# A second level of seven products in the w_out half of an attention and SiLU kernel

## The chip, the cores and the metric

The kernel runs on one core of a Trainium2 chip. The metric is the device time of one execution in microseconds (us). Executions of one kernel agree within 0.4% here (before 1540.95 to 1544.35); ratios are taken within runs that were made together on the same chip. In the profile PE is TensorE, PEld its weight loads, DVE VectorE, ACT ScalarE, POOL GpSimd, SP the engine that issues the DMAs. The granted clock is the share of TensorE's full speed that the chip allowed at a time. To evict or empty a bank is to copy a finished product out of PSUM, and an operation is held (off) when it stands still until another engine's operation ends.

## The reference

```python
# q, k, v: (8, 12, 448, 64)
q_n, k_n = rmsnorm(q, g_q), rmsnorm(k, g_k)
attn = softmax(scale * q_n @ k_n.T)             # per batch and head
x = (attn @ v).transpose(0, 2, 1, 3).reshape(3584, 768)
h = x @ w_in                                    # 768 x 2048
g = h / (1 + exp(-h))
out = g @ w_out                                 # 2048 x 768, float32
```

The change concerns the last line, and how `g` ("hidden") is stored for it.

## The kernel before: the parts that matter

Each large product is done in Winograd's form of Strassen's method: both operands are cut into four blocks, and seven block products with some sums of blocks take the place of eight. The left operand's sums are s1, s2, s4, the right one's t1, t2, t4. `seven` runs the products and adds them up as they come out of PSUM:

```python
def seven(left, right, steps, n, done):
    ...
    p1, u2, u3, p5 = (parts[:, ds(i * S, n)] for i in range(4))
    nc.scalar.copy(p1, (yield from product("1")))
    plus((yield from product("2")), p1, done[1, 1])
    plus((yield from product("6")), p1, u2)
    nc.scalar.copy(p5, (yield from product("5")))
    plus((yield from product("7")), u2, u3)
    nc.gpsimd.tensor_tensor(out=u2, in0=u2, in1=p5, op=ALU.add)
    nc.gpsimd.tensor_tensor(out=done[2, 2], in0=u3, in1=p5, op=ALU.add)
    plus((yield from product("3")), u2, done[1, 2])
    plus((yield from product("4")), u3, done[2, 1])

def bank(n):                      # a product's PSUM bank: two in turn
    return ps.tile([P, BANK], F32, name="mm", bufs=2)[:, 0:n]
```

The kernel lays out eight PSUM banks. In attention two are `mm`, one `tr`, one `av`, and four hold scores, as two tiles of two banks (one bank per head):

```python
def scores(n, half):
    for j in range(2 * half, 2 * half + 2):
        banks = ps.tile([R, 2, BANK], F32, name="sc", bufs=2)
        ...
```

The kernel has three stages. In the first (to about 860 us) attention runs pair by pair of heads, with the w_in product of the batches already done as a filler. In the second (to 1028 us) the last two batches' w_in product runs while w_out is loaded, rounded and summed (`prepare_out`). In the third, 14 tiles of 256 tokens are each multiplied with all of w_out: `left_sums`, then `seven` with 8 steps of 384 columns, then the stores.

Of the kernel before, what the change touches and what calls it, by code (L numbers as in the profile page):

```python
# [168 lines left out]
def kernel(  # L169
# [19 lines left out]



    nc = tc.nc
    z = Shapes(q, w_in)
    P, D, R, J = z.P, z.D, z.R, z.J
# [108 lines left out]
    )  # L303


def store(nc, out, z, column, o, m0):


    at = 0
    while at < o.shape[0]:  # L310
        b, c = divmod(column + at, z.S)
        j, p = divmod(c, z.R)
        n = min(z.R - p, o.shape[0] - at)
        rows = out[ds(b * z.S, z.S), ds(m0, o.shape[1])].rearrange("(p j) m -> j p m", j=z.J)
        nc.sync.dma_start(rows[j, ds(p, n)], o[ds(at, n), :])
        at += n

# [2 lines left out]
def bounded(  # L320
# [17 lines left out]
        return parts  # L338


    hidden = dram.tile([z.NF, P, z.B * S], F32, name="hidden")


    sets = [mem.tile([P, 2 * z.NW * S], F32, name=f"x{i}") for i in range(2)]
    sums_x = mem.tile([P, 3 * HW * S], F32, name="sums_x")
    NSTAGE = 3
    stage = mem.tile([P, NSTAGE * 2 * S], F32, name="stage")
    parts = mem.tile([P, 4 * S], F32, name="parts")
    work = mem.tile([P, 15 * S + 2 * J * D], F32, name="work")
    qT0, qT1, kT, e0, e1, e2, e3, es, xU, r = divided(  # L350
# [12 lines left out]
    def normalise(n):  # L363
        if n <= last:
            normalise_rows(
                nc, z, state[n], normal[n % 2], squares, rms[n % 4], minus_half, nc.gpsimd
            )
# [22 lines left out]
    def scores(n, half):  # L390

        for j in range(2 * half, 2 * half + 2):
            banks = ps.tile([R, 2, BANK], F32, name="sc", bufs=2)
            for h in range(2):
                rows = ds(h * D, D)
                nc.tensor.matmul(  # L396
                    banks[:, h, 0:S], kT[rows, ts(j, R)], qT[n % 2][rows, :],
                    start=True, stop=True,
                )
            for h in range(2):  # L400
                nc.scalar.activation(  # L401
                    e[j][:, h, :], banks[:, h, 0:S], AF.Exp, scale=rms[n % 4][:, 1, h, j : j + 1]
                )
# [35 lines left out]
    def minus(a, b, out):  # L439
        nc.vector.tensor_tensor(out=out, in0=a, in1=b, op=ALU.subtract)  # L440

    def plus(a, b, out):
        nc.vector.tensor_tensor(out=out, in0=a, in1=b, op=ALU.add)  # L443

    def left_sums(a11, a12, a21, a22, s1, s2, s4, steps=range(4)):

        for step in steps:
            (
                lambda: plus(a21, a22, s1),
                lambda: minus(s1, a11, s2),  # L450
                lambda: minus(a11, a21, a21),
                lambda: minus(a12, s2, s4),
            )[step]()

    def right_sums(b11, b12, b21, b22, t1, t2, t4):

        minus(b12, b11, t1)
        minus(b22, t1, t2)
        minus(b22, b12, b12)
        minus(b21, t2, t4)  # L460

    def bank(n):
        return ps.tile([P, BANK], F32, name="mm", bufs=2)[:, 0:n]

    def seven(left, right, steps, n, done):



        def product(name):
            t = bank(n)  # L470
            for i, s in enumerate(steps):
                nc.tensor.matmul(  # L472
                    t, left(name, s), right(name, s), start=i == 0, stop=i == len(steps) - 1
                )
                yield n
            return t

        p1, u2, u3, p5 = (parts[:, ds(i * S, n)] for i in range(4))
        nc.scalar.copy(p1, (yield from product("1")))  # L479
        plus((yield from product("2")), p1, done[1, 1])  # L480
        plus((yield from product("6")), p1, u2)
# [5 lines that stand above are left out]
        plus((yield from product("4")), u3, done[2, 1])  # L487


    stages = 0  # L490

    def staged():
        nonlocal stages
        stages += 1
        return stage[:, ts((stages - 1) % NSTAGE, 2 * S)]

    def save(f, column, t):
        nc.sync.dma_start(hidden[f, :, ds(column, t.shape[1])], t)

    def whole(b, blocks):  # L500

        for f in blocks:
            h = bank(S)
            assert room.w_in.rounded >= (f // room.CHUNK + 1) * z.NW
            for c in range(z.NW):
                nc.tensor.matmul(  # L506
                    h, room.w1(c, f), xT(b, c), start=(c == 0), stop=(c == z.NW - 1)
                )
                yield S
            t = staged()[:, 0:S]  # L510
            nc.scalar.activation(t, h, AF.Silu)
            save(f, b * S, t)

    summed = set()

# [22 lines left out]
    def halves_in(group, blocks, beside=lambda m: iter(())):  # L538
        owed = []
        for m in blocks:  # L540
# [21 lines left out]
            done = {(i + 1, j + 1): rows[i][:, ts(j, S)] for i in range(2) for j in range(2)}  # L562
            aside = beside(m)
            count = 0
            for columns in seven(lambda name, c: lefts[name](c), right, range(HW), S, done):
                count += 1
                if count % HW == 1:
                    if count > HW:
                        activate(owed)
                    next(aside, None)  # L570
                yield columns
            for _ in aside:
                pass
            owed = [(2 * m + i, group[0], rows[i]) for i in range(2)]
        activate(owed)

    def activate(owed):
        for f, b, t in owed:
            nc.scalar.activation(t, t, AF.Silu)
            save(f, b * S, t)  # L580
        owed.clear()



# [24 lines left out]
    def chunk_out(i):  # L609

        w = home[i][0].rearrange("p (m r h k) -> p m r h k", m=2, r=2, h=2)
        s = home[i][1].rearrange("p (s m k) -> p s m k", s=3, m=2)
        return (
            w[:, :, 0, 0], w[:, :, 0, 1], w[:, :, 1, 0], w[:, :, 1, 1], s[:, 0], s[:, 1], s[:, 2]
        )

    def prepare_out(m):

        if m == 0:
            fetch(0)  # L620
        for _ in range(room.CHUNK):
            rounder.open()
            yield
            rounder.round()
        if m % 2:
            right_sums(*chunk_out(ORDER[m // 2]))
        yield

    NT = z.B * S // P
    size = z.NF * 2 * P  # L630
    tiles = [work[:, ds(0, size)], sets[1][:, ds(0, size)]]
    s_tiles = [work[:, ds(size, 3 * HF * P)], sums_x[:, ds(0, 3 * HF * P)]]
    outs = [stage[:, ds(i * z.DM, z.DM)] for i in range(3)]
    outs += [room.chunk(3)[:, ts(i, z.DM)] for i in range(3)]

    def fetch(t):

        if t >= NT // 2:
            return
        dst = tiles[t % 2].rearrange("p (f c) -> p f c", f=z.NF)  # L640
        nc.sync.dma_start(
            dst, hidden[:, :, ds(t * 2 * P, 2 * P)].rearrange("f p c -> p f c")
        )

    def halves_out(t):
        w = tiles[t % 2].rearrange("p (m r t c) -> p m r t c", m=HF, r=2, t=2)
        s = s_tiles[t % 2].rearrange("p (s m c) -> p s m c", s=3, m=HF)
        a11, a12, a21, a22 = (w[:, :, i, j] for j in range(2) for i in range(2))
        left_sums(a11, a12, a21, a22, s[:, 0], s[:, 1], s[:, 2])
        lefts = {"1": a11, "2": a12, "3": s[:, 2], "4": a22, "5": s[:, 0], "6": s[:, 1], "7": a21}  # L650

        def right(name, m):
            b11, b12, b21, b22, t1, t2, t4 = chunk_out(m // 2)
            return {"1": b11, "2": b21, "3": b22, "4": t4, "5": t1, "6": t2, "7": b12}[name][
                :, m % 2
            ]

        o = [outs[(2 * t + i) % len(outs)] for i in range(2)]
        done = {(i + 1, j + 1): o[i][:, ts(j, z.HALF)] for i in range(2) for j in range(2)}
        steps = [2 * i + k for i in ORDER for k in range(2)]  # L660
        yield from seven(lambda name, m: lefts[name][:, m], right, steps, z.HALF, done)
        for i in range(2):
            if t < NT // 2 - 1 or i == 0:
                store(nc, out, z, (2 * t + i) * P, o[i], 0)
            else:
                for j in (1, 0):
                    store(nc, out, z, (2 * t + i) * P, o[i][:, ts(j, z.HALF)], j * z.HALF)


    filler = dict(work=iter(()), due=0.0, share=0.0)  # L670

    def begin(work, columns, parts):
        finish()
# [11 lines left out]
    def finish():  # L685
        for _ in filler["work"]:
            pass
# [34 lines left out]
    for n in range(last + 2):  # L722
# [40 lines left out]
            fill()  # L763
        weights_in(n, 3)
        normalise(n + 3)
    finish()
    fetch(1)
    for t in range(NT // 2):
        for _ in halves_out(t):
            pass  # L770
        fetch(t + 2)


@with_exitstack
# [208 lines left out]
```

## Time and profile before

| | us |
|---|---|
| median of 9 runs, over all comparisons | 1543.4 (1540.95 to 1544.35) |
| profiled run: span | 1539.4 |
| start of the last reciprocal but one of attention | 859.1 |
| first matmul of the third stage | 1027.7 |
| end of its last matmul | 1533.7 |

The three last rows are read from the instructions in order of time, and they cut the span into four stretches: attention (859.1), preparation (168.6), w_out product (506.0) and end (5.7). The lines behind this are shown in the prediction.

### The profile page before, as it was taken

To read this page: it belongs to the slowest core of one execution; us is meant where nothing else is said; L and a number is where in the kernel's file an instruction comes from. 1 tells how busy PE (TensorE), PEld (TensorE's weight loads), DVE (VectorE), ACT (ScalarE), POOL (GpSimd) and SP (SyncE) were. 2 spreads that over 40 slices of the span, in tenths; PEclk is the share of its full clock that TensorE was granted. 3 is DMA by queue.
4 is the path that set the end of the run, shared out by engine and by line. 5 is a ranking of instruction groups with operands and counts; after the bars stand their busy time and mean duration, and the time that the engine had idled before them with its cause. 6 is when DMAs were issued, how large, how long until landed. Compare 5 with 4: busy or idle time off the path is not lost.

```text
span 1539.4 us, 13964 instructions
## 1 busy us (share of the span) xinstructions
PE 1460.6 (95%) x5048; PEld 706.8 (46%) x5048; DVE 739.7 (48%) x939; ACT 562.9 (37%) x928; POOL 379.9 (25%) x243
## 2 busy tenths in 40 slices
PE   4899999999899999899999689999999999999998
PEld 1234344434344444344444244445555555555554
DVE  3887776765755545755555465651121112121221
ACT  4779877554455455445545324320000000000000
POOL 4455442433333323332331033320000000000000
PEclk9999999999999999999999889999999999999999
DMA  6424432221222122222211334542222222222220
GB/s 200 107 62 133 123 96 64 62 65 59 60 60 84 54 68 77 60 60 78 66 48 60 117 99 141 159 138 75 75 75 76 75 76 75 75 76 86 75 86 24
DMA packets 119187, 128.94 MB, mean 84 GB/s; under 512 B 48836, under 2 KB 101316, under 8 KB 119108
## 3 DMA queue, kind: packets, MB, share of 16 engines
q1 hardware_dynamic: 118784, 127.95, 27.4%
q8 instruction: 42, 0.69, 0.2%
q14 instruction: 37, 0.30, 0.1%
q10 hardware_dynamic: 324, 0.00, 0.0%
HBM read 87.56 MB, written 40.37 MB: 83 GB/s over the span
## 4 chain that ended last, share of the span: by engine, by line
PE 86%; DVE 8%; DMA 3%; ACT 1%; issue 1%; POOL 0%; SPq 0%; ACTq 0%; DVEq 0%; POOLq 0%
PE mm L472 57%; PE sc L396 10%; PE av L412 9%; PE mm L506 5%; PE tr L433 3%; DVE work L423 2%; PE tr L382 2%; DMA rows<-in_moe_w_out_dram 2%; DVE sums_x L440 1%; PE tr L377 1%; DVE rms L292 1%; DMA rows<-in_k_dram 1%; DVE W L440 1%; DMA W<-in_moe_w_in_dram 0%; DVE x L440 0%
## 5 line engine op out<-in xcount | busy, mean ns | idle before, releaser
L401 ACT ACTIVATE work<-sc,rms 112x448 f32<-112x448 f32 x384 | 212.3, 635 | 227.0 <-PE sc L396 146.7
L472 PE MATMUL mm<-x,W 128*128 128x448 f32 x672 | 267.7, 542 | 1.3 <-DVE stage L443 0.9
L297 POOL TENSOR_TENSOR rms<-rms,minus_half 112x16 f32<-112x16 f32 x48 | 175.2, 3650 | 341.3 <-DVE rms L294 338.6
L472 PE MATMUL mm<-sums_x,W 128*128 128x448 f32 x504 | 212.6, 559 | 31.1 <-DVE parts L443 13.1
L472 PE MATMUL mm<-W,work 128*128 128x384 f32 x588 | 197.6, 486 | 0.0
L484 POOL TENSOR_TENSOR parts<-parts 128x448 f32<-128x448 f32 (+1 forms) x42 | 45.6, 1085 | 611.0 <-DVE parts L443 611.0
L434 DVE RECIPROCAL work<-tr 128x448 f32<-128x448 f32 x48 | 142.0, 2957 | 109.5 <-PE tr L433 109.5
L396 PE MATMUL sc<-work 64*112 64x448 f32 x768 | 174.0, 573 | 7.3 <-ACT work L386 4.9
L443 DVE TENSOR_TENSOR stage<-mm,parts 128x448 f32<-128x448 f32 (+1 forms) x109 | 66.1, 608 | 238.2 <-PE mm L472 144.9
L472 PEld LDWEIGHTS mm<-x,W 128*128 128x128 f32 x672 | 125.0, 191 | 117.1 <-issue 109.7
L443 DVE TENSOR_TENSOR parts<-mm,parts 128x448 f32<-128x448 f32 (+1 forms) x84 | 50.4, 600 | 254.6 <-PE mm L472 254.3
L412 PE MATMUL av<-work,rows 112*64 112x448 f32 x768 | 165.8, 553 | 0.0
L423 DVE TENSOR_TENSOR work<-work 112x896 f32<-112x896 f32 x144 | 159.3, 1106 | 1.9
L479 ACT COPY parts<-mm 128x448 f32<-128x448 f32 (+1 forms) x42 | 21.8, 518 | 358.6 <-PE mm L472 358.6
L472 PEld LDWEIGHTS mm<-sums_x,W 128*128 128x128 f32 x504 | 94.7, 195 | 125.5 <-issue 77.7
L472 PEld LDWEIGHTS mm<-W,work 128*128 128x128 f32 x588 | 111.7, 190 | 77.9
L482 ACT COPY parts<-mm 128x448 f32<-128x448 f32 (+1 forms) x42 | 21.6, 515 | 250.7 <-PE mm L472 250.7
L472 PE MATMUL mm<-W,x 128*128 128x384 f32 x336 | 112.9, 486 | 0.0
L396 PEld LDWEIGHTS sc<-work 64*112 64x112 f32 x768 | 62.4, 176 | 107.8 <-issue 90.9
L412 PEld LDWEIGHTS av<-work,rows 112*64 112x64 f32 x768 | 46.8, 136 | 109.9 <-issue 107.7
L472 PE MATMUL mm<-W,sums_x 128*128 128x384 f32 x252 | 84.7, 486 | 0.0
L472 PEld LDWEIGHTS mm<-W,x 128*128 128x128 f32 x336 | 63.8, 190 | 44.5
(72 smaller groups left out, 1383.7 us busy)
## 6 DMA issues: line engine op xcount, KB each, us to landing
hidden<-stage SPq DMA_DIRECT2D x56, 448.0 KB, 2.8
work<-hidden SPq DMA_DIRECT2D x7, 2048.0 KB, 9.0
x<-hidden SPq DMA_DIRECT2D x7, 2048.0 KB, 9.3
W<-in_moe_w_in_dram SPq DMA_DIRECT2D x24, 512.0 KB, 4.3
rows<-in_moe_w_out_dram SPq DMA_DIRECT2D x32, 384.0 KB, 3.6
rows<-in_q_dram SPq DMA_DIRECT2D x48, 224.0 KB, 3.6
rows<-in_k_dram SPq DMA_DIRECT2D x48, 224.0 KB, 3.4
rows<-in_v_dram SPq DMA_DIRECT2D x48, 224.0 KB, 2.7
```

The costliest lines, as they stand in the source:

```text
L297: nc.gpsimd.tensor_tensor(out=flat, in0=flat, in1=minus_half[0 : z.R].to_broadcast([z.R, 4 * z.J]), op=ALU.pow)
L382: nc.tensor.transpose(t[:, ts(j, R)], rows[:, j].rearrange("p h d -> p (h d)"), ident[0:R, 0:R])
L396: nc.tensor.matmul(banks[:, h, 0:S], kT[rows, ts(j, R)], qT[n % 2][rows, :], start=True, stop=True,)
L401: nc.scalar.activation(e[j][:, h, :], banks[:, h, 0:S], AF.Exp, scale=rms[n % 4][:, 1, h, j : j + 1])
L412: nc.tensor.matmul(st["av"][ds(h * D, D), :], st["v"][:, h, j, :], e[j][:, h, :], start=(j == 0), stop=(j == J - 1),)
L423: nc.vector.tensor_tensor(out=es, in0=e[0] if j == 1 else es, in1=e[j], op=ALU.add)
L433: nc.tensor.matmul(t[ds(h * D, D), :], ones[0:R, :], es[:, h, :], start=True, stop=True)
L434: nc.vector.reciprocal(out=r, in_=t)
L443: nc.vector.tensor_tensor(out=out, in0=a, in1=b, op=ALU.add)
L472: nc.tensor.matmul(t, left(name, s), right(name, s), start=i == 0, stop=i == len(steps) - 1)
L484: nc.gpsimd.tensor_tensor(out=u2, in0=u2, in1=p5, op=ALU.add)
L506: nc.tensor.matmul(h, room.w1(c, f), xT(b, c), start=(c == 0), stop=(c == z.NW - 1))
```

## The change

The intent: apply the seven products a second time. The outer level cuts tokens and features of hidden, and features and outputs of w_out, in halves; it makes seven passes over all tokens, one per outer product; a pass has seven rounds (one tile of tokens each), and a round is an inner `seven` with 4 steps of 192 columns. What an outer product gives to the four output quarters is kept in SBUF until the pass that completes it. Hidden is stored as four quarters (a11, a12, s2 = a21 + a22 - a11, a22); the three other left operands are formed by GpSimd from two of them. The preparation is cut into 14 small steps, all eight PSUM banks are used once attention is over, and w_out's first loads are issued one head pair sooner. Cut to its core:

```diff
-    hidden = dram.tile([z.NF, P, z.B * S], F32, name="hidden")
+    TOKENS = z.B // 2 * S
+    hidden = dram.tile([4, HF, P, TOKENS], F32, name="hidden")
...
-            banks = ps.tile([R, 2, BANK], F32, name="sc", bufs=2)
+            banks = ps.tile([P, 2, BANK], F32, name="sc", bufs=2)[0:R]
...
     def bank(n):
-        return ps.tile([P, BANK], F32, name="mm", bufs=2)[:, 0:n]
+        if not alone:
+            return ps.tile([P, BANK], F32, name="mm", bufs=2)[:, 0:n]
+        if not free_banks:
+            for name in ("mm", "mm", "tr", "av"):
+                free_banks.append((name, [P, S if name in ("tr", "av") else BANK], None))
+            for _ in range(2):
+                free_banks.extend(("sc", [P, 2, BANK], i) for i in range(2))
+        name, shape, half = free_banks.pop(0)
+        if half != 1:
+            shared["bank"] = ps.tile(shape, F32, name=name, bufs=2 if name in ("mm", "sc") else 1)
+        t = shared["bank"]
+        return t[:, 0:n] if half is None else t[:, half, 0:n]
...
+    def third(a11, a21, a22):
+        nc.gpsimd.tensor_tensor(out=a21, in0=a21, in1=a22, op=ALU.add)
+        nc.gpsimd.tensor_tensor(out=a21, in0=a21, in1=a11, op=ALU.subtract)
...
+    PASSES = "1265374"
+    SOURCES = {      # stored quarter, second stored quarter, how they combine
+        "1": (0, None, None), "2": (1, None, None), "6": (2, None, None), "4": (3, None, None),
+        "5": (2, 0, ALU.add), "3": (1, 2, ALU.subtract), "7": (3, 2, ALU.subtract),
+    }
+    rounds = [(k, t) for k in range(len(PASSES)) for t in range(NT)]
...
+    def combine(n, half):
+        ...
+                nc.gpsimd.tensor_tensor(out=a, in0=a, in1=b, op=op)   # 128x1024, two a round
...
+    def beside_out(n, point):      # what runs beside the inner product number `point`
+        if point == 0:
+            fetch(n + 2)
+            for half in range(2):
+                combine(n + 1, half)
+                fetch_other(n + 2, half)
+        if point == 1:
+            finish_out(n - 1)
+        ...
+        if n == last:
+            while rounder.load():
+                pass
+            alone = True
+            stages.append(spare)
     finish()
     fetch(1)
-    for t in range(NT // 2):
-        for _ in halves_out(t):
-            pass
-        fetch(t + 2)
+    for n in range(len(rounds)):
+        products_out(n)
+    finish_out(len(rounds) - 1)
```

## The prediction

> **What bounds the kernel now.** I read the page's head, then the granted clock, then busy time by stretches, then TensorE's groups with their shapes, and last the instructions in order of time where TensorE stops. TensorE carries nearly everything, so the first view only says where to look:
>
> ```profile
> span 1539.4 us, 13964 instructions
> PE 1460.6 (95%) x5048; PEld 706.8 (46%) x5048; DVE 739.7 (48%) x939; ACT 562.9 (37%) x928; POOL 379.9 (25%) x243
> ```
>
> The change rewrites the w_out product, which is the last third of the span. Busy time by stretches: in 400 us there TensorE never stops, at clock 1.00, while VectorE, ScalarE and GpSimd idle and the DMA engines are a quarter busy (columns: stretch, length, PE, PEld, DVE, ACT, POOL, clock, DMA share, GB/s).
>
> ```profile
> 1100.00:1500.00 400.00, 400.00 (x1242) 235.61 (x1241) 83.93 (x102) 10.54 (x22) 21.45 (x22) 1.00 0.26 80
> ```
>
> But 100% busy by itself doesn't say that columns are the limit; overlapped records hide the real pace. The pace is read from the order in time:
>
> ```profile
> 1199.74 3.71 PE L472 MATMUL mm<-W,work 128*128 128x384 f32 x11
> 1203.29 1.45 PE L472 MATMUL mm<-x,work 128*128 128x384 f32 x4
> ```
>
> Eleven matmuls from 1199.74 to the next start at 1203.29: 0.3227 us each. 384 columns at 2.4 GHz with two clocks a column would be 320 ns, so 2.7 ns are overhead. (A float32 product is two instructions here: 14 tile pairs x 7 products x 8 steps = 784 products make 1568 instructions of 384 columns in the by-shape groups; each instruction is 2 clocks a column.) The group's "486 ns of one" is a latency with a tail that overlaps the next; it is not the cost. From the first of them at 1027.70 to 1533.7 the stage lasts 506.0 us = 1568 x 0.3227.
>
> Just before it lies a stage in which w_out is loaded and prepared beside the last group of the w_in product. There TensorE does stop (the bracket is the idle time before, and its releaser):
>
> ```profile
> 871.18 1.76 PE L433 MATMUL tr<-work,ones 112*64 112x448 f32 x4 [2.62 <-DVE work L423]
> 881.99 3.35 PE L472 MATMUL mm<-sums_x,W 128*128 128x448 f32 x4 [9.05 <-ACT parts L479]
> 887.68 5.19 PE L472 MATMUL mm<-sums_x,W 128*128 128x448 f32 x8 [2.33 <-DVE sums_x L440]
> ...
> 916.21 4.85 PE L472 MATMUL mm<-sums_x,W 128*128 128x448 f32 x6 [3.05 <-DVE parts L443]
> ...
> 954.04 2.52 PE L472 MATMUL mm<-sums_x,W 128*128 128x448 f32 x6 [3.04 <-DVE parts L443]
> ...
> 988.92 2.52 PE L472 MATMUL mm<-sums_x,W 128*128 128x448 f32 x6 [3.05 <-DVE parts L443]
> ...
> 1023.80 4.11 PE L472 MATMUL mm<-sums_x,W 128*128 128x448 f32 x6 [3.04 <-DVE parts L443]
> ```
>
> The 9.05 us are named for a ScalarE copy, but that copy stands in ScalarE's queue behind the first step of w_out's rounding, which waited 14.79 us for its load. The load was issued at 871.52, right behind the 2 MB fetch of the first hidden tile at 871.09:
>
> ```profile
> 871.09 0.38 SPq L641 DMA_DIRECT2D work<-hidden  x1
> ...
> 871.52 3.14 SPq L67 DMA_DIRECT2D rows<-in_moe_w_out_dram  x3
> ...
> 880.54 0.54 ACT L82 ACTIVATE rows<-rows 128x384 int32<-128x384 uint32 x1 [14.79 <-DMA rows<-in_moe_w_out_dram]
> ```
>
> The four stalls of 3.04 us come where VectorE builds the column sums of a w_out chunk in one go (four operations, partly waiting for GpSimd's rounding) while both PSUM banks of the product wait to be emptied.
>
> **What the Trainium skill says.** (1) "TensorE: Matmul & The Clock Gate", section "Back-to-back issue gap": N/2.4 + 2.5 ns for an isolated warm matmul, but in a stream of weight loads and matmuls both set the pace, and small N is undercounted. The trace agrees with the first at two clocks a column (322.7 ns); no shape in it tests the second at N = 192. (2) Same page, "LDWEIGHTS (loading the stationary operand)": columns / 1.2 ns, so 107 ns for 128 columns, against 190 ns recorded. The trace's loads are 136, 176 and 190 ns for 64, 112 and 128 columns: 0.84 ns a column, which is the page's rate, plus 83 ns of latency. (3) "GPSIMD Engine Reference", "Specifications": GpSimd shares its SBUF interfaces with VectorE and contends with VectorE instructions that read two SBUF inputs. The trace agrees: GpSimd's addition of 128x384 takes 1.01 us alone and 1.56 us at 911.33, under a VectorE addition of 128x768. No page speaks of this algorithm.
>
> **The change part by part.**
> 1. Fewer columns. The seven products are applied twice: 7 outer passes x 7 tiles x 7 inner products x 4 steps = 1372 products of 192 columns in place of 784 of 384; the built program lists 1372. In instructions 2744 of 192 columns for 1568 of 384: columns fall to 7/8, the number of instructions and weight loads rises by 1.75. If the pace stays columns plus overhead, one costs 160 + 2.7 = 162.7 ns, and the stage is 2744 x 0.1627 = 446.5 us, 59.5 less than 506.0.
> 2. Does a load fit under 162.7 ns? This is the step on which everything hangs, for the recorded 190 ns is longer. Two views speak for it. First, the four key transposes (columns: start, duration):
>
> ```profile
> 26.18 0.39 PEld L382 LDWEIGHTS tr<-ident,rows 112*128 112x128 f32 x4 [0.70 <-ACT work L401]
> 26.19 0.60 PE L382 MATMUL tr<-ident,rows 112*128 112x112 f32 x4
> ```
>
> Loads of 142 ns each, four in 0.39 us: they start (390 - 142)/3 = 83 ns apart, so a load's record does not block the next. Second, a chain after an idle stretch with the full-size load:
>
> ```profile
> 263.38 0.30 PEld L472 LDWEIGHTS mm<-x,W 128*128 128x128 f32 x2 [1.00 <-ACT stage L511]
> ```
>
> Two 190 ns loads in 0.30 us: the second begins 0.11 us after the first. So a load holds the path for about 110 ns and the rest is latency; 110 is under 160, and the load stays hidden.
> 3. The other engines in the new stage. A round (one tile of one pass) lasts 56 x 0.1627 = 9.1 us. VectorE: four tile sums of 128x512 (1.22 us for 1024 elements now, so about 0.6 each, 2.4), five evictions of 192 columns (about 0.3 each, 1.5), on average one addition of 128x768 to the kept partial result (0.9), and in four rounds of seven column sums of 192 (4 x 0.25): some 5.4 us, 60%. GpSimd: 2 x 0.57 us in every round, and in the passes 5, 3 and 7, whose left operand is two stored quarters combined, 2 more operations of 128x1024 (0.99 us for 384 and 1.13 for 448 give 2.2 ns an element: 2.4 each): 5.9 us, with contention 8 to 9.5. DMA: 1 MB a round, 2 MB in those three passes, plus 0.4 MB stores in passes 2, 3, 7, 4: at worst 2.5 MB in 9.1 us = 273 GB/s. The 2048 KB fetches now take 9.0 to 9.3 us and the 384 KB loads 3.6, hence some 300 GB/s behind 2.3 us of latency. It fits, narrowly. Fetches run two rounds ahead and evictions have eight banks instead of two. I charge 8 us over the 21 rounds of the three passes.
> 4. First loads a pair sooner and ahead of the hidden fetch. The ScalarE copy is no longer held. Lost there now: 2.62 + 9.05 + 2.33 idle, and 12 matmuls from 881.99 to 892.71 that took 10.7 us, of which 2.33 idle and 4.5 needed: 3.9 at a lowered clock; 17.9 in all. What stays is the wait for the last pair's reciprocal (2.97), product (0.63) and sums (1.2), some 5 us less what TensorE can do meanwhile, the 2.62, and a slower clock after it: 8. Saved 10.
> 5. Preparation in fourteen small steps, with all eight banks in use in the last group: the four stalls (12.2), the slow restart at 916.21 (4.85 for 2.4) and 1.4 us before 1027.70, in sum 16, should fall to 3. Saved 13.
> 6. Added elsewhere: hidden is stored as four quarters, the third being a sum made by GpSimd, two operations of 1.13 us for each of 32 blocks, 72 us on an engine that is 25% busy; the bytes stored stay the same. The end gains one VectorE operation (0.9). I charge 2 us.
>
> Sum: 1541.6 - 59.5 - 10 - 13 + 8 + 2 = 1469 us.
>
> **The rivals.** (a) The load becomes the bound. If the next matmul must wait for the whole recorded load, each takes at least 190 ns: 2744 x 0.190 = 521 us, the stage loses 15 us, the preparation still gains 23, and the kernel ends near 1540: same. For it: no float32 stream this short is in the trace, and the first warning of the skill's page on small N. Against it: the two load views. (b) GpSimd or DMA becomes the bound in passes 5, 3 and 7. At 11 us a round, 21 rounds lose 40 us: about 1500. For it: 5.9 us of GpSimd work that stretches under VectorE, and a single buffer for the second quarter, filled in halves only after the previous half is consumed. Against it: both fit in 9.1 us, and TensorE has a round of slack in banks. (c) The stalls of the preparation only move, for VectorE still waits there for loads, ScalarE and GpSimd in order: 1482. (d) GpSimd's third quarter delays the normalisation of the pairs, and attention loses some us: 1475 to 1480. GpSimd waits for VectorE most of that time, which speaks against it.
>
> **Range and chances.** Part 1 is exact if part 2 holds; parts 3 to 6 are uncertain by some 15 us. Rival (b) stretches the upper end. Range 1453 to 1500. Faster by over 2% means below 1510.8: only rival (a), or a heavy (b) with (c), prevents it. Faster 0.91, same 0.06, slower 0.03.
>
> **What would show it.** In order of time, 192-column matmuls 163 ns apart with loads still recorded at about 190 ns would show part 2 right; 190 ns apart, rival (a). In busy time by round, passes 1, 2, 6, 4 at 9.1 us with TensorE full; if passes 5, 3, 7 are longer, TensorE's idle brackets name GpSimd or a hidden fetch for rival (b). Between attention and the new stage the 9.05 us bracket should be gone, and the 3.04 ones with it, else (c). Before 850 us the busy shares should hardly move, else (d). A paced stream above 170 ns would make the prediction wrong more than all else.

## The result

The changed kernel takes 1631.8 us (median of 4, 1630.3 to 1636.2) against 1541.7 of the kernel before in the same rounds: ratio 1.059, 95% interval 1.057 to 1.061, slower. The forecast was 1469, range 1453 to 1500.

The head of the changed kernel's page:

```profile
span 1628.5 us, 17662 instructions
PE 1451.8 (89%) x6224; PEld 875.0 (54%) x6224; DVE 1041.4 (64%) x1415; ACT 581.1 (36%) x998; POOL 615.0 (38%) x419
```

TensorE is no longer full. The ledger by stretch, each number read from the two traces (spans, in us; the predicted column puts each saving of the forecast at its stretch and is scaled to the span, 2 us under the time):

| stretch | before | predicted | changed |
|---|---|---|---|
| attention, to the last reciprocal but one | 859.1 | 860.2 | 871.4 |
| preparation, to the first 192-column matmul | 168.6 | 145.6 | 170.2 |
| w_out product, to the end of its last matmul | 506.0 | 454.5 | 579.1 |
| end | 5.7 | 6.6 | 7.8 |
| sum | 1539.4 | 1466.9 | 1628.5 |

Three stretches fail, and the large one is the product. A piece of TensorE's order in time in a pass that combines nothing, with VectorE and ScalarE of the same 5 us (three answers):

```profile
1150.58 1.57 PE L493 MATMUL sc<-rows,work 128*128 128x192 f32 x8 [0.59 <-DVE rows L447]
1151.98 0.49 PE L493 MATMUL sc<-x,W 128*128 128x192 f32 x2
1152.31 1.14 PE L493 MATMUL sc<-W 128*128 128x192 f32 x6
1153.91 0.59 PE L493 MATMUL sc<-x,W 128*128 128x192 f32 x2 [0.46 <-ACT parts L500]
```

```profile
1150.16 0.36 DVE L447 TENSOR_TENSOR rows<-sc,parts 128x192 f32<-128x192 f32 x1 [0.48 <-POOL parts L505]
```

```profile
1153.54 0.32 ACT L500 COPY parts<-sc 128x192 f32<-128x192 f32 x1 [5.72 <-PE sc L493]
```

Read it so. Within a product the pace is 163 ns (the eight matmuls of the product at 1151.98 start 1.14 us apart from first to last, in seven steps): the weight loads are hidden, as part 2 of the prediction had it. But the product at 1150.58 starts right after VectorE emptied a bank `sc`, and the one at 1153.91 right after ScalarE did. What ScalarE copies from 1153.54 is the product that ran from 1151.98, the one just before. So of four products in `sc` banks every second one waits until its predecessor has been emptied, while older banks stand free. Worked out from the starts of all matmuls in passes 2, 6 and 4: the product in the second half of a two-bank tile starts 0.61 to 1.85 us late, median 0.65, and at the other six places in the cycle of eight banks none starts even 0.01 us late.

The preparation, which uses the same eight banks, stops at the same place. From 890 us to the first 192-column matmul it has fourteen stops over 0.3 us, 20.5 us in sum, and every one stands before a product in an `sc` bank; one of them:

```profile
917.02 2.42 PE L493 MATMUL sc<-x,W 128*128 128x448 f32 x6
922.59 3.73 PE L493 MATMUL sc<-sums_x,W 128*128 128x448 f32 x6 [3.14 <-DVE stage L447]
```

Over all 49 rounds (start of one round's first matmul to that of the next, the last one to the end of its last matmul, worked out from the trace) it looks like this:

```
pass (tiles 0..6), us a round                            sum
"1"  16.18 10.06 10.86  9.99 10.55 10.64 10.54          78.8
"2"  10.76 10.67 10.06 10.86  9.99 10.55 10.63          73.5
"6"  10.54 10.76 10.67 10.34 10.87  9.99 11.78          75.0
"5"  15.25 14.90 11.29 15.19 12.17 13.05 11.45          93.3
"3"  12.45 15.24 14.84 11.29 14.63 12.52 13.05          94.0
"7"  11.61 15.12 16.24 15.88 11.07 11.08 10.03          91.0
"4"  10.86  9.98 10.55 10.63 10.54 10.89  9.98          73.4
```

A plain round takes 10.5 us in place of 9.1; passes 5, 3 and 7, which combine quarters, 13.3. What happens in those is seen in GpSimd and VectorE, from 1374 us on:

```profile
1374.22 5.54 POOL L746 TENSOR_TENSOR work<-work,sums_x 128x1024 f32<-128x1024 f32 x2
```

```profile
1374.73 2.83 DVE L444 TENSOR_TENSOR sums_x<-W,sums_x 128x512 f32<-128x512 f32 x1
1377.49 0.34 DVE L447 TENSOR_TENSOR W<-tr,parts 128x192 f32<-128x192 f32 x1
1377.94 2.64 DVE L447 TENSOR_TENSOR W<-W,work 128x768 f32<-128x768 f32 x1
```

A VectorE addition of 128x512, 0.68 us elsewhere, lasts 2.83, and one of 128x768 lasts 2.64 instead of 0.96. GpSimd's two operations, 2.77 us each, end at 1377.02 and 1379.76, and the two additions end 0.55 and 0.82 us after that, not much less than they take alone: they stand still until GpSimd is done and run then. The eviction between them, which reads PSUM and one SBUF operand, takes its usual 0.34 us.

Attention loses 12.3 us in jumps where the column sums of a two-batch group's input are made. There, before, TensorE idled 1.11 us ahead of a sum over the scores; now 2.99. Kernel before:

```profile
401.32 0.97 PE L433 MATMUL tr<-work,ones 112*64 112x448 f32 x4 [1.11 <-DVE work L423]
```

Changed kernel (one place later in time, the same instruction; then what stands on GpSimd and VectorE ahead of it):

```profile
406.92 0.97 PE L437 MATMUL tr<-work,ones 112*64 112x448 f32 x4 [2.99 <-DVE work L427]
```

```profile
397.96 1.61 POOL L522 TENSOR_TENSOR stage<-stage 128x448 f32<-128x448 f32 x1 [9.44 <-ACT stage L620]
...
398.48 1.56 DVE L444 TENSOR_TENSOR sums_x<-x,sums_x 128x448 f32<-128x448 f32 x1
...
399.64 1.39 POOL L523 TENSOR_TENSOR stage<-stage 128x448 f32<-128x448 f32 x1
399.97 1.55 DVE L444 TENSOR_TENSOR sums_x<-x 128x448 f32<-128x448 f32 x1
```

Two of VectorE's column sums, 0.62 us each elsewhere, take 1.56 and 1.55 under GpSimd's two operations for the third quarter: together 1.87 us, which is the growth of TensorE's stop (2.99 - 1.11 = 1.88). After this stop the granted clock fell to half, for two windows of 3.4 us (from 408.3 and from 418.6). The comparison of the reciprocals, pair by pair (counted from 0), shows jumps of 1.9 us at pairs 16, 23 and 35, of 3.3 and 1.6 us at pairs 24 and 36, right after the last two stops, and of 0.7 and 0.8 us at pairs 1 and 11.

### The profile page after: what moved, and what is told of

The parts are those of the page before. It is cut to its first block, busy times and chain, and to the rows that moved or that the text cites. A ratio compares the mean times of both kernels' runs of the same rounds, so it can differ in the third digit from the quotient of the medians.

```text
span 1628.5 us, 17662 instructions
## 1 busy us (share of the span) xinstructions
PE 1451.8 (89%) x6224; PEld 875.0 (54%) x6224; DVE 1041.4 (64%) x1415; ACT 581.1 (36%) x998; POOL 615.0 (38%) x419
## 4 chain that ended last, share of the span: by engine, by line
PE 67%; DVE 15%; issue 8%; POOL 5%; ACT 2%; DMA 1%; ACTq 0%; POOLq 0%; DVEq 0%
PE mm L493 24%; PE sc L493 12%; PE sc L400 9%; PE av L416 8%; PE mm L531 4%; PE tr L437 3%; POOL W L746 2%; PE tr L493 2%; DVE work L427 2%; DVE sums_x L444 2%; PE av L493 2%; DVE work L444 2%; PE tr L386 2%; DVE stage L447 1%; POOL parts L505 1%
## 5 line engine op out<-in xcount | busy, mean ns | idle before, releaser
L505 POOL TENSOR_TENSOR parts<-parts 128x192 f32<-128x192 f32 (+1 forms) x77 | 76.7, 997 | 496.8 <-DVE parts L447 496.8
L493 PE MATMUL mm<-x,W 128*128 128x448 f32 (+1 forms) x588 | 226.3, 520 | 1.3 <-DVE stage L447 0.9
L493 PE MATMUL mm<-sums_x,W 128*128 128x448 f32 x396 | 165.2, 552 | 9.4 <-DVE stage L447 5.4
L493 PEld LDWEIGHTS mm<-sums_x,W 128*128 128x128 f32 x396 | 73.4, 193 | 78.7 <-issue 60.8
L493 PE MATMUL sc<-x,W 128*128 128x192 f32 (+1 forms) x214 | 75.2, 461 | 33.7 <-DVE stage L447 10.9
L522 POOL TENSOR_TENSOR stage<-stage 128x448 f32<-128x448 f32 x28 | 35.0, 1252 | 156.0 <-ACT stage L620 124.2
L444 DVE TENSOR_TENSOR W<-W 128x192 f32<-128x192 f32 (+2 forms) x122 | 77.8, 653 | 0.9
L493 PE MATMUL sc<-W,work 128*128 128x192 f32 x378 | 78.0, 346 | 0.0
L493 PE MATMUL sc<-x,work 128*128 128x192 f32 x126 | 36.3, 372 | 44.4 <-DVE parts L447 29.2
L746 POOL TENSOR_TENSOR W<-W,sums_x 128x1024 f32<-128x1024 f32 x28 | 75.9, 2732 | 0.0
```

The costliest lines, as they stand in the source:

```text
L444: nc.vector.tensor_tensor(out=out, in0=a, in1=b, op=ALU.subtract)
L493: nc.tensor.matmul(t, left(name, s), right(name, s), start=i == 0, stop=i == len(steps) - 1)
L746: nc.gpsimd.tensor_tensor(out=a, in0=a, in1=b, op=op)
```

## The experiments

Theory A: (1) two products that share a two-bank tile are made to wait for each other by the program, not by the chip; (2) GpSimd's operations hold off VectorE's two-input operations for their whole length, in passes 5, 3, 7 and at the ends of the groups. Rivals: VectorE is too slow for its share of work; eight banks are too few; the DMA traffic is the limit in passes 5, 3 and 7. A run's state (fast, or slow in a disturbed execution) is told from several runs side by side: times below of a single run have an unknown state, and where runs were timed in rounds, all were fast.

### Four tiles of one bank (e1_single_banks)

```diff
-            banks = ps.tile([P, 2, BANK], F32, name="sc", bufs=2)[0:R]
+            banks = [ps.tile([P, BANK], F32, name="sc", bufs=4)[0:R, 0:S] for _ in range(2)]
...
-            for name in ("mm", "mm", "tr", "av"):
-                free_banks.append((name, [P, S if name in ("tr", "av") else BANK], None))
-            for _ in range(2):
-                free_banks.extend(("sc", [P, 2, BANK], i) for i in range(2))
...
+            for name in ("mm", "mm", "tr", "av", "sc", "sc", "sc", "sc"):
+                free_banks.append((name, [P, S if name in ("tr", "av") else BANK]))
```

> The changed kernel, but the four PSUM banks of the attention scores are taken as four tiles of one bank instead of two tiles of two. Theory A (the built program makes the product in the second half of such a tile wait for the emptying of the first half, so TensorE waits two times in eight products): the waits of 0.6 to 0.7 us at every second 'sc' product vanish, the 28 rounds without a combination fall from 10.5 to about 9.15 us, the preparation before the stage gets some 15 to 20 us shorter, and the whole falls from 1631 to about 1525 to 1555 us. Rival B (VectorE, with 7 us of work a round plus waits, is simply too slow to empty the banks): the plain rounds stay at 10.3 to 10.6 us, the waits move to other banks, the whole stays above 1615 us.

Measured: right result, 1506.2 us (1502.1 to 1506.7, 4 runs), ratio to the kernel before 0.976 (0.974 to 0.978). Plain rounds are 9.10 us to the last digit. TensorE in one of them:

```profile
1100.91 1.46 PE L489 MATMUL sc<-rows,W 128*128 128x192 f32 x8
1102.21 0.49 PE L489 MATMUL mm<-x,W 128*128 128x192 f32 x2
1102.54 1.14 PE L489 MATMUL mm<-W 128*128 128x192 f32 x6
1103.51 0.49 PE L489 MATMUL mm<-x,W 128*128 128x192 f32 x2
1103.84 1.14 PE L489 MATMUL mm<-W 128*128 128x192 f32 x6
1104.81 1.46 PE L489 MATMUL tr<-rows,work 128*128 128x192 f32 x8
```

No brackets: from 1102.21 to 1104.81 sixteen matmuls, 162.5 ns each. Theory A(1) holds, and more follows than I had expected, because the preparation had used the same banks: it falls from 170.2 to 143.3 us, the product from 579.1 to 478.9. From 893 us to the end of the preparation TensorE no longer stops for over 0.3 us; four products in `sc` banks in a row, without a bracket:

```profile
953.77 4.67 PE L489 MATMUL sc<-x,W 128*128 128x448 f32 x12
958.28 4.67 PE L489 MATMUL sc<-sums_x,W 128*128 128x448 f32 x12
```

The effect is larger than the sum I wrote down (1525 to 1555), I take it (not tested apart) because with independent banks TensorE also runs ahead through a good part of VectorE's holds: passes 5, 3 and 7 fall from 278 to 211 us in sum. The first two rounds don't gain: 18.9 and 11.8 us.

### Six banks, no two products in one tile (e6_six_banks)

```diff
-                free_banks.extend(("sc", [P, 2, BANK], i) for i in range(2))
+                free_banks.append(("sc", [P, 2, BANK], 0))
```

> The changed kernel with only the first half of each two-bank tile used, so six banks in rotation and no two products in one tile. Theory A (the wait is for the other half of the same tile, not for lack of banks): the plain rounds fall to 9.1 us with fewer banks than the changed kernel has, the whole to about 1505 to 1530 (rounds of passes 5, 3 and 7 somewhat longer than the mean of 10.1 with eight single banks, for there is less slack under VectorE's 2.7 us waits). Rival B (banks are short, and single tiles gave more freedom): plain rounds at 10.5 us or above, the whole above 1610.

Measured: right result, 1504.2 us (one run); plain rounds 9.10 us, the product 479.7 us in all. The tiles are still of two banks, but the second is unused, and the kernel is as fast with six banks as with eight. So it is neither the number of banks nor the shape of the tile: it is two products in one tile. In the changed kernel's built program the matmul that opens the second half of such a tile indeed carries a semaphore wait on the engine that empties the first. (In all 85 places where a product of 192 columns goes into such a second half, the wait is for the very instruction that empties the first half.) Lines of the list of TensorE's instructions in the built program, two tiles of it:

```
1131 L493 Matmult sc_5019<-work_144,W_75 128x192 [waits DVE_49]
1133 L493 Matmult sc_5019<-x0_139,work_144 128x192 [waits DMAHW1_49,DVE_49]
1135 L493 Matmult sc_5033<-x0_139,work_144 128x192
1137 L493 Matmult sc_5033<-work_144,sums_x_141 128x192 [waits DVE_49]
```

### No combination in passes 5, 3 and 7 (e2_no_combine)

```diff
-                nc.gpsimd.tensor_tensor(out=a, in0=a, in1=b, op=op)
+                pass
```

> The changed kernel without GpSimd's additions of two stored quarters in passes 5, 3 and 7; all fetches stay (the result is wrong on purpose). Theory A (a GpSimd operation of 128x1024 with two SBUF inputs holds VectorE's two-input operations off until it ends, some 4 us a round): the 21 rounds of these passes fall from a mean of 13.3 to about 10.5 us, as in the plain passes, VectorE's 128x512 and 128x768 operations of 2.6 to 2.8 us there go back to 0.7 and 1.0, and the whole falls by 55 to 60 us to about 1574. Rival B (the doubled fetches of 2.5 MB a round are the limit): these rounds stay above 12.5 us and the whole above 1610.

Measured: wrong result; 1577.5 us (one run). The passes fall from 93.3, 94.0 and 91.0 to 73.5, 74.1 and 73.3 us, the level of the plain ones, and VectorE's operations there are back at 0.68 and 0.96 us: from 1060 us on none of 190 and 49 lasts over 1 us, where in the changed kernel 26 of 188 and 16 of 49 last over 1.5. One group of them, from 1270 to 1450 us (columns: count, then busy us and mean ns of one):

```profile
L444 DVE TENSOR_TENSOR sums_x<-W,sums_x 128x512 f32<-128x512 f32 x6 | 4.1, 682 | 0.0
```

All the fetches are still made. The rival with the DMA traffic falls.

### Copies in place of the additions (e4_copy_combine)

```diff
-                nc.gpsimd.tensor_tensor(out=a, in0=a, in1=b, op=op)
+                nc.gpsimd.tensor_copy(out=a, in_=b)
```

> The changed kernel with GpSimd's additions in passes 5, 3 and 7 replaced by copies of the second quarter, of the same size and at the same place but with one input (wrong result on purpose). Theory A1 (it is the second SBUF input that makes the two engines exclude each other): VectorE's operations there are back at 0.7 and 1.0 us, the rounds at 10.5 to 11 us, the whole at 1574 to 1585. Rival A2 (any GpSimd operation on SBUF holds VectorE off): VectorE's operations stay stretched to the length of the copy, the rounds stay above 11.5 us.

Measured: wrong result; 1581.2 us (one run), passes 77.7, 78.3 and 75.8 us. A GpSimd and two VectorE groups, the latter from 1270 to 1450 us (columns: count, then busy us and mean ns of one):

```profile
L746 POOL COPY W<-sums_x 128x1024 f32<-128x1024 f32 x28 | 39.3, 1432 | 0.0
```

```profile
L444 DVE TENSOR_TENSOR sums_x<-W,sums_x 128x512 f32<-128x512 f32 x6 | 9.1, 1518 | 0.0
L444 DVE TENSOR_TENSOR work<-W,work 128x512 f32<-128x512 f32 x5 | 7.6, 1518 | 0.0
```

Rival A2 has the mechanism right, as far as this copy goes, and not my A1: under a copy with one input, 1.43 us long, VectorE's addition of 128x512 takes 1.52 us instead of 0.68. It costs little because the copy is half as long: a round of these passes takes 11.0 us in the mean, below A2's 11.5. The whole lies in A1's range all the same, so the total could not have told the two apart; the durations did.

### The third quarter on VectorE (e3_third_on_vector)

```diff
-        nc.gpsimd.tensor_tensor(out=a21, in0=a21, in1=a22, op=ALU.add)
-        nc.gpsimd.tensor_tensor(out=a21, in0=a21, in1=a11, op=ALU.subtract)
+        nc.vector.tensor_tensor(out=a21, in0=a21, in1=a22, op=ALU.add)
+        nc.vector.tensor_tensor(out=a21, in0=a21, in1=a11, op=ALU.subtract)
```

> The changed kernel with the third quarter computed by VectorE instead of GpSimd (two operations a block). Theory A (GpSimd's two operations hold up VectorE's column sums of the input at the ends of the groups, TensorE stands still 1.9 us longer there and the clock drops after it): the last attention pair but one starts within 4 us of the kernel before instead of 12.4 us later, the waits of 1.55 us of VectorE there are gone, the whole falls by 6 to 10 us to about 1622 to 1626. Rival B (the added 36 us of VectorE work delay the same places as much): no change within 3 us.

Measured: right result, 1636.0 us (one run); the last pair but one 18.2 us later than before, not 12.4. My forecast missed, and rival B's "no change within 3 us" is nearer (5.8 us later than in the changed kernel at that pair, 4.2 in the whole): the two operations stand in VectorE's own queue ahead of the same column sums, so they delay them too. At that place VectorE is no better than GpSimd; whether the position is what matters is tried below with the late third quarter.

### No third quarter (e5_single_no_third)

Single-bank tiles, and `third` does nothing.

> Single-bank tiles, and GpSimd's two operations for the third quarter left out (wrong result on purpose). Theory A (at the ends of the groups these operations hold up the column sums of the input on VectorE, and the stop drops the clock): the last attention pair but one, now 14.5 us later than in the kernel before, is at most 4 us later, and the whole falls by 8 to 12 us to about 1494 to 1498. Rival B (the delay comes from something else, the order of the stores or the two-bank rows): still 10 us or more later, the whole above 1502.

Measured: wrong result; 1480.4 us (one run), 14 us below theory A's range. The last pair but one is 1.8 us later than before, against 14.5 with single banks alone, and the first two rounds are 11.0 and 9.2 us. So the third quarter's operations are the whole loss of attention but 1.8 us, and also the 10 us of the first rounds, which I hadn't counted: there they and their store stand ahead of the next hidden tile's fetch. (Runs with the same attention code put this pair 10 to 15 us late, 10.1 to 15.0 in six profiles; the spread goes roughly with the time at half clock before 875 us: 20.5 us of it in the runs with 10.1 and 12.4, 30.7 in the one with 15.0. Differences under 5 us are not read here.)

### The third quarter late, the second fetch early (e7_late_third)

```diff
+        if group[0] == z.B - 2:
+            fetch(1)
         activate(owed)
-        settle(owed)
+        late_sums.append(owed)
...
         normalise(n + 3)
+        while late_sums:
+            settle(late_sums.pop())
...
     finish()
-    fetch(1)
+    settle(late_sums.pop())
```

> Single-bank tiles; at the end of a group the third quarter is computed after the next pair's normalisation instead of before the input's column sums, and the second hidden tile is fetched before the last stores instead of behind them (right result). Theory A: the delay of attention falls from 14.5 to about 4 to 6 us, the first two rounds of the stage from 30.7 to about 20 to 23 us, the whole from 1506 to about 1486 to 1492. Rival B (the last group's own chain on VectorE, not the fetch, holds the first rounds): first two rounds stay at 26 us or more, the whole 1496 to 1500.

Measured: right result, 1490.2 us (1489.0 to 1491.2), ratio 0.966 (0.965 to 0.968). The pair is 5.6 us late, the first two rounds take 22.7 us: both in theory A's ranges. The jumps at pairs 23 and 35 are gone, by the position alone; the one at pair 16, whose third quarter was not moved, stays (3.5 us).

### All seven left operands stored (e8_seven_stored)

GpSimd forms the seven operands block by block while attention runs; the stage combines nothing.

```diff
-    hidden = dram.tile([4, HF, P, TOKENS], F32, name="hidden")
+    hidden = dram.tile([7, HF, P, TOKENS], F32, name="hidden")
...
+        tt(out=a21, in0=a21, in1=a22, op=ALU.add);       save(5, m, g, a21)
+        tt(out=a11, in0=a21, in1=a11, op=ALU.subtract);  save(2, m, g, a11)
+        tt(out=a12, in0=a12, in1=a11, op=ALU.subtract);  save(4, m, g, a12)
+        tt(out=a22, in0=a22, in1=a11, op=ALU.subtract);  save(6, m, g, a22)
```

> As the late third, but GpSimd forms all seven left operands while attention runs (four operations a block instead of two) and stores them; the stage fetches 1 MB a round throughout and combines nothing. Theory A (GpSimd's 128x1024 additions are what stretches passes 5, 3 and 7): all rounds from the third on at 9.10 us, 20 us less in the stage; attention pays 2 to 8 us for the doubled GpSimd work; the whole at about 1470 to 1480. Rival B (the additions under attention hold VectorE off so often that TensorE stops there): attention more than 20 us later than in the kernel before, the whole at or above 1490.

Measured: right result, 1491.6 us (1490.5 to 1494.4), ratio 0.967 (0.966 to 0.969). Theory A's first half holds: from the third round on every one of the 47 is 9.10 us. Its total is missed and lies in rival B's range, though without B's sign (over 20 us late): the pair is 13.7 us late, and the first round takes 23.6 us, because TensorE waits for VectorE, which waits for GpSimd's four operations:

```profile
1025.02 1.24 PE L489 MATMUL tr<-work 128*128 128x192 f32 x6 [1.03 <-DVE stage L447]
1036.97 1.01 PE L489 MATMUL tr<-work 128*128 128x192 f32 x2 [10.71 <-DVE work L444]
```

The work moved off one stage is paid back in the two others.

### The combination on VectorE (e9_combine_on_vector)

As the late third, with one word changed:

```diff
-                nc.gpsimd.tensor_tensor(out=a, in0=a, in1=b, op=op)
+                nc.vector.tensor_tensor(out=a, in0=a, in1=b, op=op)
```

> As the late third (1490 us), with the additions of the stored quarters in passes 5, 3 and 7 on VectorE instead of GpSimd (right result). VectorE is then 7.0 + 2 x 1.22 = 9.4 us busy a round, and nothing is held off. Theory A (what stretches these rounds is that VectorE's own operations stand still while GpSimd's 2.4 us operations run): VectorE's 128x512 and 128x768 operations there return to 0.7 and 1.0 us, the 21 rounds fall from a mean of 10.1 to about 9.5 us, the whole to about 1477 to 1483. Rival B (the amount of work on VectorE is the limit, whoever causes it): the rounds go to 10.5 us or more and the whole to 1498 or more.

Measured: right result, 1470.0 us (1466.9 to 1471.1), ratio 0.953 (0.951 to 0.954): the fastest of all, ahead of the kernel before and the changed one. All rounds from the second on are 9.10 us, better than theory A's 9.5. Busy time from 1213 to 1404 us, the three combining passes (columns as in the prediction), and VectorE's new groups there:

```profile
1213.00:1404.00 191.00, 191.00 (x1177) 191.00 (x1177) 165.25 (x299) 13.37 (x42) 30.39 (x42) 1.00 0.77 244
```

```profile
L746 DVE TENSOR_TENSOR W<-W,sums_x 128x1024 f32<-128x1024 f32 x26 | 30.5, 1209 | 0.0
L746 DVE TENSOR_TENSOR work<-work,sums_x 128x1024 f32<-128x1024 f32 x12 | 14.1, 1209 | 0.0
```

TensorE full, at clock 1.00, with VectorE 165/191 = 87% busy and the DMA engines 77% busy at 244 GB/s. More work on VectorE made VectorE faster, since the holds it suffered were longer than the work: two operations of 1.21 us in place of about 4 us of standing still a round (2.83 - 0.68 and 2.64 - 0.96 above). That settles both remaining rivals: neither VectorE's amount of work nor the traffic was the limit.

### The loads not sooner (e10_late_loads)

On the single-bank kernel, the part "first loads a pair sooner" undone:

```diff
-            while rounder.load():
-                pass
             alone = True
```

> Single-bank tiles, without the part 'w_out's first loads a pair sooner': they are issued when the first piece is opened. Theory A (what removed the 9 us stop is that the first product's copy stands ahead of the rounding in ScalarE's queue and that the 2 MB fetch is no longer ahead of the load; issuing a pair sooner adds little, for the loads now land some 5 us before TensorE starts again): the whole within 4 us of the 1506 with single banks. Rival B (the earlier issue is what removed it): a wait of 4 us or more for the load returns before the last group, and the whole is 1511 to 1518.

Measured: right result, 1503.3 us (1499.8 to 1505.4), against 1506.2 with the part: no difference to be read. Why is in the issuing queue. Changed kernel first, this run second:

```profile
880.87 0.32 SPq L518 DMA_DIRECT2D hidden<-stage  x1
881.25 17.77 SPq L67 DMA_DIRECT2D rows<-in_moe_w_out_dram  x6
```

```profile
880.05 0.32 SPq L514 DMA_DIRECT2D hidden<-stage  x1
880.42 17.73 SPq L67 DMA_DIRECT2D rows<-in_moe_w_out_dram  x6
```

In both the load goes out right behind a store of hidden (in the single-bank kernel, from which this run differs by the one edit, at 883.41 behind a store at 883.04). In the program it stood a pair earlier; in time it did not, for the queue stood at the store, which waits for GpSimd's third quarter. It doesn't matter: the 9.05 us stop is gone in both, since the first product's copy now stands ahead of the rounding on ScalarE and the 2 MB fetch behind the loads.

## Why the prediction was wrong

Parts 1 and 2 (the pace; the step on which "everything hangs") were right: 162.5 ns against 162.7, and 49 x 9.10 = 446 us is what the product takes once nothing else stands in its way (with the combination on VectorE: 450.5 with a slow first round). Rival (a) is out. Of the two views for it the first was weaker than the prediction thought: the key transposes' loads have 128 columns too and are recorded at 142 ns, so they don't fit the rate that it read from the others (190 ns for 128) and are of another kind.

The step that failed is part 5's and part 3's "all eight banks": "evictions have eight banks instead of two", "with all eight banks in use in the last group: the four stalls ... should fall to 3". I counted banks and didn't ask what the program guards as one. Four of the eight came in tiles of two, and the second product of a tile waited for the emptying of the first. None of the four rivals names this wait. Cost, by the single-bank run: 100.1 us in the product (579.06 - 478.95) and 26.9 in the preparation (170.2 - 143.3). With that taken away the preparation gains 168.6 - 143.3 = 25.3 us, and the forecast was 23. This could have been seen before any run, in the waits of the built program.

Part 3, the combining passes: the mechanism was half right and mis-sized. I let VectorE stretch GpSimd's operations; it is mostly the other way round, and whole operations are held. Its own line could have told: the GpSimd addition from 911.33 ended at 912.89, 0.86 us after VectorE's (911.08 + 0.95), so it had waited rather than shared. Charged 8 us; with single banks they cost 211.5 - 21 x 9.10 = 20.4, in the changed kernel 278.3 - 21 x 10.5 = 58, and on VectorE nothing. So rival (b), "GpSimd or DMA becomes the bound", was in the right place with the wrong limit: neither is; VectorE is late with its evictions and sums, held off by GpSimd. The first two rounds stood in no part of the sum: with single banks they take 30.7 us, 12.5 more than two plain ones.

Part 6, attention: charged 2 us with rival (d), measured 12.3, of which the run without the third quarter leaves 1.8. I had looked at how busy GpSimd is (25%), where the question was what stands still beside it: the column sums at the ends of the groups lie on TensorE's path.

Part 4: 10 forecast, and attention's loss shrinks by 8.7 us between the last two reciprocals (12.36 to 3.64 us late), so the size was right. The reason that gave the part its name was not: the earlier issue adds nothing.

Rival (c), stalls that only move, describes the changed kernel's preparation well (170.2 us), but its reason, loads and engines in order, wasn't the cause. The numbers of the sum fit what the chip does without the two faults: 1469 forecast, 1470.0 measured with single banks, a late third quarter and the combination on VectorE. That agreement is partly luck, as attention still loses 6.9 us and the first round 4.4 there, against 8 that I charged to the combination.

Attention's 12.4 us divide by the jumps: 5.65 in the three stops, 4.9 at pairs 24 and 36, and 1.5 at pairs 1 and 11, where the run without the third quarter loses as much (1.65). In the stretch of pair 24 lie two windows of half clock of 3.4 us and in that of pair 36 one, none of them in the kernel before; at half speed a window loses 1.7 us (an estimate from its length), so they account for the 4.9. What stays open: why the end is 2.1 us longer (0.9 forecast). The added VectorE operation is 0.96 of it; the rest wasn't looked into.

## What to carry to other kernels

Before counting on more PSUM banks, look in the built program at what each product's first matmul waits for: two products in halves of one tile may be guarded as one, and a tile per bank cost nothing here. Before moving elementwise work to an idle GpSimd, ask which two-input VectorE operations run at that time, for here they stood still until it was done; moving 2.4 us of work onto the busier engine can shorten the round. And judge a busy share by what stands beside it: an engine at 25% can still put 12 us on the path.

## What the Trainium skill lacked or had wrong

- "SBUF — State Buffer", "SBUF: two separate sides", says that VectorE and GpSimd share a port pair under an exclusive lock: the loser blocks for the whole instruction. A VectorE 128x512 addition of 0.68 us took 2.83 under a GpSimd addition of 2.77, and 1.52 under a one-input copy of 1.43, while evictions from PSUM kept 0.34. The prediction rested on "GPSIMD Engine Reference", "Specifications", which only says "contention" and doesn't point there; on its own it led to a term of 8 us where 58 were lost (20.4 with single banks).
- "PSUM — Partial Sum Buffer", "PSUM bank collisions raise a hardware error", says that accesses to different banks run clean, so the wait of the second half of a two-bank tile is none of the chip's. No page says that a built program may guard such a tile as one: a median of 0.65 us at every second product in it in the plain passes, 127 us in this kernel with all that followed.
- "TensorE: Matmul & The Clock Gate", "Back-to-back issue gap", warns that in a stream of weight loads and matmuls small N is undercounted by N/2.4 + 2.5 ns. It gives no float32 stream. With two instructions a product and a weight load of 128 columns before each, 192 columns ran at 162.5 ns, that is 2N/2.4 + 2.5: at this length the warning did not apply, though the loads were recorded at 190 ns (median).
